# Attention followed by a mixture of experts on one core: tokens as 64 x 9 with 64x64 tiles, engine orders from a list scheduler, experts in three phases

## The chip, the core and the metric

The kernel runs on one core of a Trainium2 chip (trn2). The metric is device time of one execution in microseconds (us), median of the runs. TensorE (PE in the profile, PEld for its weight loads) multiplies matrices, VectorE (DVE), ScalarE (ACT) and GpSimd (POOL) work on tiles, and SyncE (SP) starts transfers. ACT and POOL start transfers too. Inputs lie in DRAM as float32.

## What is computed

```python
def reference(q, k, v, w_gate, w1, w2, capacity):       # q, k, v: [8, 8, 576, 64]
    theta = np.pi / 2 * np.arange(576) / 576
    phi = lambda x: concat(relu(x) * cos(theta), relu(x) * sin(theta))     # 128 features
    kv = einsum('bhsf,bhsd->bhfd', phi(k), v)
    z = phi(k).sum(axis=2)
    num = einsum('bhsf,bhfd->bhsd', phi(q), kv)
    den = einsum('bhsf,bhf->bhs', phi(q), z) + 1e-6
    x = (num / den).transpose(0, 2, 1, 3).reshape(4608, 512)
    logits = x @ w_gate                                  # 8 experts
    e, g = argmax(logits), softmax(logits)[argmax]
    # the first `capacity` (1152) tokens of an expert are kept, in order of the tokens
    out[i] = g[i] * (relu(x[i] @ w1[e[i]]) @ w2[e[i]])   # w1: [8, 512, 1024], w2: [8, 1024, 512]
```

## The kernel before

**Attention and routing.** A pass `it` of the loop at L627 weaves streams of steps that belong to different batches: `stage_a(it)` (L230), `stage_p(it - 1)` (L329) and `stage_r(it - 2)` (L353). `run` (L82) gives every step of a stream a place between two fractions of the pass and issues all steps in the order of these places. This, and nothing measured, sets the order on every engine.

The 576 tokens of a batch are 4 chunks of 128 partitions and a tail of 64. k, v and q are loaded by SP, each as a 128-partition part and a tail (`load`, L187). `stage_a` takes the relu of k on ACT (L242), multiplies v by cos and sin into `vs` (DVE at L257, ACT at L254), transposes the relu of q on TensorE (`q_ps`, L272) and copies the result with ACT to `rq` (L274). `kv_pair` (L291) sums k·v over the 5 chunks, two heads at a time, one in each half of the array's columns:

```python
nc.tensor.matmul(out=kv_v[o * D:(o + 1) * D, w % 2, :, :], lhsT=lhsT, rhs=rhs,          # L301
                 start=(c == 0), stop=(c == NC - 1))
```

k·v is copied to `kvt` and `kva` (L304, L305), turned (L313), multiplied by the gate's weights (`g_ps`, L322) and put beside k·v in `kva`, so that the next product gives attention, denominator and logits at once. `stage_p` does this product in 10 units of a batch, four matmuls each (`p_ps`, L339); ACT takes the cos half times `costab` into `tmp` (L344), DVE adds the sin half times `sintab` into `num` (L346). `p_ps` has two buffers. `stage_r` is a chain of some 20 small DVE operations (denominator, logits, maximum, softmax, one-hot `oh`), with a count of tokens by expert on TensorE (`c_ps`, L434 to L444), and ends in `slot_i`, the row of each token in the DRAM table `xd`, sorted by expert. `emit` (L491) scales `num` into `xg` (3 of 5 chunks on DVE, 2 on POOL) and `scatter` (L500) writes the rows by indirect DMA from POOL.

**Experts.** A table of blocks of 128 rows of one expert is made on DVE: `table_a` after 7 batches for 24 blocks, `table_b` after the last for 19 (L590, L608). `table_b` also makes ACT start 8 small DMAs that write zero rows behind each expert's rows (L614), each after loading a register from `end_i`. `fetch` (L661) reads a block with a transposing DMA (L666) and its token numbers (L668). `up` (L675) multiplies by one half of w1 (`w1a` or `w1b`), ACT takes the relu into `h` (L685), `turn` (L688) transposes `h` on TensorE and DVE copies it to `hT` (L695), `down` (L697) multiplies by w2 (`w_sb`), DVE or ACT copies `y` (two buffers), and POOL scatters its rows to the output (L716).

The halves `w1a` are loaded during attention (`w1_piece`, L517). `w1b` and w2 lie where the attention pools were, and are loaded by POOL after those pools are released (L645) and after the last batch's scatters in POOL's order (L731 to L734). Seven blocks do their first half of `up` while the last batch is routed; the other blocks follow in the loop at L744, which does both `up` halves and both turns of block i and the `down` of block i - 17 in one round. The last 17 `down` stand alone at the end.

## Time and profile before

| what | value |
|---|---|
| median of 3 runs | 463.3 us (461.96 to 466.05) |
| profiled execution | 467.96 us |
| its span in the trace | 466.2 us |
| busy: PE, DVE, ACT, POOL | 344.4, 182.4, 191.6, 130.0 us |
| mean granted clock of TensorE | 0.871 of 2.4 GHz |

The profile is of one execution. Busy time is the union of an engine's instructions; matmuls are pipelined and their ends are modelled, so the distance between starts says more than a duration. In a timeline row the first number is the start, the second the length of the merged stretch, `x8` the number of instructions, and the brackets hold the idle time before it and what ended it. A float32 matmul is two instructions in the trace, so one unit of P is `x8`.

### The profile page before, as it was taken

What the parts mean: (1) busy time and instruction counts of PE and PEld (TensorE: products, weight loads), DVE (VectorE), ACT (ScalarE), POOL (GpSimd) and SP (SyncE); (2) the same over time, 40 slices, a digit from 0 to 9 for tenths busy, and PEclk for the clock granted to TensorE, in tenths of its full rate; (3) what the DMA queues carried; (4) which work ended last, traced back from release to release, by engine and by line L of the source; (5) the groups of instructions that cost most, each with busy time, mean ns of one, the idle gap of its engine ahead of it and who ended that gap; (6) DMA issues with size and microseconds to landing.
All of it is one profiled execution on the core that took longest, in us unless ns stands there. A gap on an engine that the chain in (4) does not pass through costs nothing.

```text
span 466.2 us, 8117 instructions
## 1 busy us (share of the span) xinstructions
PE 344.4 (74%) x2651; PEld 219.6 (47%) x2672; DVE 182.4 (39%) x528; ACT 191.6 (41%) x367; POOL 130.0 (28%) x157
## 2 busy tenths in 40 slices
PE   0079779798988878956560049753999999999984
PEld 0066557576767666754220024431455555555331
DVE  1131356746575757548490002210223232323221
ACT  1064776756757676632110015431343434342110
POOL 3000001615160617256075320000222222223444
PEclk9986997959797989885575559998899999999999
DMA  1975472867877774452249999999455332111220
GB/s 25 337 249 167 140 226 80 252 150 211 192 230 172 221 181 79 73 102 65 64 113 172 213 207 188 186 197 175 93 123 105 103 103 79 69 69 70 99 93 35
DMA packets 91560, 66.55 MB, mean 143 GB/s; under 512 B 46077, under 2 KB 88061, under 8 KB 91520
## 3 DMA queue, kind: packets, MB, share of 16 engines
q0 software_dynamic: 22000, 30.96, 30.7%
q1 hardware_dynamic: 68368, 34.01, 29.5%
q10 hardware_dynamic: 1152, 1.05, 0.8%
q8 instruction: 24, 0.39, 0.4%
q14 instruction: 16, 0.13, 0.1%
HBM read 61.92 MB, written 17.06 MB: 169 GB/s over the span
## 4 chain that ended last, share of the span: by engine, by line
PE 49%; DMA 20%; DVE 8%; issue 7%; ACT 7%; POOL 3%; SPq 3%; another core or an unknown queue 1%; POOLq 0%; DVEq 0%; ACTq 0%
PE h_ps L683 13%; PE kv_ps L301 10%; PE y_ps L704 10%; PE p_ps L339 8%; DMA xT<-xd 7%; DMA w1b<-in_moe_w_dram 5%; DMA out_dram<-y,ix 4%; PE ht_ps L694 3%; DVE num L346 2%; ACT vs L254 2%; PE q_ps L272 2%; ACT tmp L344 2%; DMA qm<-in_q_dram 2%; PE g_ps L322 2%; DMA qt<-in_q_dram 2%
## 5 line engine op out<-in xcount | busy, mean ns | idle before, releaser
L685 ACT ACTIVATE h<-h_ps 128x512 bf16<-128x512 f32 x86 | 51.3, 598 | 120.3 <-PE h_ps L683 103.2
L704 PE MATMUL y_ps<-w_sb,hT 128*128 x333 | 80.5, 385 | 11.4 <-DMA w_sb<-in_moe_w_dram 6.6
L339 PE MATMUL p_ps<-kva,rq 64*128 64x146 f32 (+1 forms) x640 | 75.2, 353 | 8.8 <-DVE num L346 6.8
L695 DVE COPY hT<-ht_ps 128x512 bf16<-128x512 bf16 x86 | 33.0, 420 | 120.6 <-PE ht_ps L694 111.7
L683 PEld LDWEIGHTS <-xT 128*128 128x128 bf16 x344 | 34.4, 101 | 72.3 <-issue 28.2
L346 DVE SCALAR_TENSOR_TENSOR num<-p_ps,sintab,tmp 128x292 f32<-128x292 f32 (+1 forms) x80 | 41.3, 518 | 69.5 <-ACT tmp L344 63.8
L339 PEld LDWEIGHTS p_ps<-kva,rq 64*128 64x128 f32 (+1 forms) x640 | 55.0, 212 | 22.5 <-DVE num L346 12.5
L683 PE MATMUL h_ps<-w1a,xT 128*128 x166 | 47.4, 406 | 15.9 <-DMA xT<-xd 10.6
L495 POOL TENSOR_TENSOR xg<-num,rden 128x512 bf16<-128x512 f32 x16 | 18.0, 1128 | 144.3 <-DVE rden L488 144.1
L716 POOL DMA_INDIRECT out_dram<-y,ids x24 | 23.4, 975 | 122.6 <-DVE y L710 87.6
L683 PE MATMUL h_ps<-w1b,xT 128*128 x168 | 45.1, 391 | 16.8 <-issue 16.6
L344 ACT ACTIVATE tmp<-p_ps,costab 128x292 f32<-128x292 f32 (+1 forms) x80 | 40.1, 501 | 40.4 <-PE p_ps L339 37.3
L704 PEld LDWEIGHTS <-hT 128*128 128x128 bf16 x344 | 32.9, 99 | 47.2 <-issue 14.5
L503 POOL DMA_INDIRECT xd<-xg,slot_i x40 | 44.3, 1108 | 22.7 <-DVE xg L495 13.7
L301 PE MATMUL kv_ps<-vs,km 128*64 128x130 f32 x512 | 43.7, 322 | 1.7 <-ACT vs L254 1.7
L272 PE MATMUL q_ps<-ident,qr 128*128 128x128 f32 x128 | 25.1, 334 | 23.4 <-DVE qr L214 23.4
L694 PE MATMUL ht_ps<-identb,h 128*128 128x128 bf16 x344 | 28.4, 224 | 14.3 <-ACT h L685 14.3
L301 PEld LDWEIGHTS kv_ps<-vs,km 128*64 128x64 f32 x512 | 34.3, 162 | 8.2 <-issue 4.8
L694 PEld LDWEIGHTS <-h 128*128 128x128 bf16 x344 | 24.0, 100 | 27.5 <-ACT h L685 15.4
L710 DVE COPY y<-y_ps 128x512 f32<-128x512 f32 x22 | 15.2, 692 | 49.7 <-PE y_ps L704 28.8
L708 ACT COPY y<-y_ps 128x512 f32<-128x512 f32 x21 | 12.3, 587 | 48.6 <-DMA out_dram<-y,ix 25.1
L272 PEld LDWEIGHTS q_ps<-ident,qr 128*128 128x128 f32 x128 | 17.7, 172 | 25.9 <-issue 23.7
(142 smaller groups left out, 329.9 us busy)
## 6 DMA issues: line engine op xcount, KB each, us to landing
km<-in_k_dram SPq DMA_DIRECT2D x8, 1024.0 KB
vm<-in_v_dram SPq DMA_DIRECT2D x8, 1024.0 KB
qm<-in_q_dram SPq DMA_DIRECT2D x8, 1024.0 KB
w_sb<-in_moe_w_dram POOLq DMA_DIRECT2D x8, 1024.0 KB
w1a<-in_moe_w_dram POOLq DMA_DIRECT2D x8, 512.0 KB
w1b<-in_moe_w_dram POOLq DMA_DIRECT2D x8, 512.0 KB
xd<-zrow ACTq DMA_DIRECT2D x8, 128.5 KB
kt<-in_k_dram SPq DMA_DIRECT2D x8, 128.0 KB
```

The lines of the kernel that those rows point to most:

```text
L272: nc.tensor.transpose(out=q_ps[:, j, :], in_=qr[:, w, j, :, :].rearrange("p o d -> p (o d)"), identity=ident[:])
L301: nc.tensor.matmul(out=kv_v[o * D:(o + 1) * D, w % 2, :, :], lhsT=lhsT, rhs=rhs, start=(c == 0), stop=(c == NC - 1))
L339: nc.tensor.matmul(out=p_ps[0:rows, o, r, 0:2 * KW], lhsT=rq[o * D:(o + 1) * D, 2 * u + r, c * P:c * P + rows], rhs=kva[o * D:(o + 1) * D, ...
L344: nc.scalar.activation(out=tmp[0:rows], in_=p_v[0:rows, :, 0:KW], func=ACT.Copy, scale=costab[0:rows, c:c + 1])
L346: nc.vector.scalar_tensor_tensor(out=num[0:rows, c, u * HB:(u + 1) * HB, :], in0=p_v[0:rows, :, KW:2 * KW], scalar=sintab[0:rows, c:c + 1] ...
L503: si = nc.gpsimd.indirect_dma_start(out=xd[:, :], out_offset=bass.IndirectOffsetOnAxis(ap=slot_i[0:rows, c:c + 1], axis=0), in_=xg[0:rows, ...
L683: nc.tensor.matmul(out=h_ps[:], lhsT=bl["xT"][:, g, :], rhs=w1h[n][:, bass.ds(e1, 1), g, :], start=(g == 0), stop=(g == G - 1))
L685: nc.scalar.activation(out=h[:], in_=h_ps[:], func=ACT.Relu)
L694: nc.tensor.transpose(out=t_ps[:, f, :], in_=bl["h", n][:, f * P:(f + 1) * P], identity=identb[:])
L695: nc.vector.tensor_copy(out=bl["hT"][:, n * (FB // 2):(n + 1) * (FB // 2), :], in_=t_ps[:])
L704: nc.tensor.matmul(out=y_ps[:], lhsT=bl["hT"][:, f, :], rhs=w2_sb[:, bass.ds(e2, 1), f, :], start=(f == 0), stop=(f == FB - 1))
L716: oi = nc.gpsimd.indirect_dma_start(out=out[:, :], out_offset=bass.IndirectOffsetOnAxis(ap=idx, axis=0), in_=y[:], in_offset=None, bounds_ ...
```

## The change

**Layout.** A batch is 64 partitions x 9 consecutive tokens (`J = 9`), and the two halves of the 128 partitions hold two heads. A load row is 9 tokens of one head, 2304 bytes; there is no tail. SP loads v, then k, then q, each in two halves, and `wg_sb` goes to ACT's queue.

**k·v.** The contraction is over 64 partitions and the output has 64 rows, so a matmul uses a quarter of the array; the four heads of a half batch take the four quarters in turn, 9 steps each, 72 matmuls (144 instructions) for a batch in place of 40 (80).

**P.** Still 10 units of four matmuls. The factor cos is divided out: ACT copies the cos half unscaled, DVE adds the sin half times tan, and the 1e-6 is scaled by 1/cos. There are three buffers of two banks for P and k·v, three for `tmp`, two single banks for the rest, two buffers each for `vs`, `rq`, `kva`, `num`, `xg` and the routing tiles, and three for `y`.

**Order.** Every step becomes an `op` of a `Plan` with engine, cost, reads, writes, buffers and a priority. `schedule` simulates the engines with these written costs and takes, on the engine that can start first, the ready op of least priority within a window; table `PHI` shifts the priority by kind of step. The program is emitted in the order found.

**Experts.** The fetch is a plain DMA of 128 rows (`xr`, 4 buffers) which TensorE transposes (`xturn`) and DVE copies (`xT`); POOL copies the token numbers (`ids`). Phase one is `xturn`, `up` with `w1a` and `turn` of all 43 blocks, phase two `up` with `w1b` and `turn`, phase three all 43 `down`. w2 is in two halves: the first is loaded with `w1b` once the last P is through (`swap`), the second into the place of `w1a`, once phase one is done.

```diff
-            m = pl.tile([P, H, NJ, D], FP32, name=name + "m", tag=name + "m")
-            t = pl.tile([D, H, D], FP32, name=name + "t", tag=name + "t")
-            nc.sync.dma_start(out=m[:], in_=src[b, :, 0:NJ * P, :].rearrange("h (p j) d -> p h j d", j=NJ))
-            nc.sync.dma_start(out=t[:], in_=src[b, :, NJ * P:S, :].rearrange("h p d -> p h d"))
+        src = srcs[name][b].rearrange("(u c o) (p j) d -> u (o p) c (j d)", u=2, o=2, j=J)[u]
...
+            nc.sync.dma_start(out=m.rearrange("p c j d -> p c (j d)"), in_=src)
+        op("SP", 0.5, f, w=[(name, b, u)], vers=[vm], prio=b - 1.2, dma=1.55).tag = ("load", name, b, u)
...
+        def kv_half(u):
+            def f():
+                kv_v = kv_tile()
+                for j in range(J):
+                    for c in range(2):
+                        for o in range(2):
+                            nc.tensor.matmul(out=kv_v[c * D:(c + 1) * D, o, u, :, :],
+                                             lhsT=loaded[b, "k", u].tile[o * D:(o + 1) * D, c, j, :],
+                                             rhs=vs_t[vs.slot][o * D:(o + 1) * D, 2 * u + c, j, :, :],
+                                             start=(j == 0), stop=(j == J - 1))
...
+            op("PE", 2.0, kv_half(u), r=[("rk", b, u)] + [("vs", b, j) for j in range(J)], w=[("kvps", b)],
+               vers=[kv, kva, loaded[b, "k", u], vs], prio=pr, mode="quad").tag = ("KV", b, u)
...
+                nc.scalar.copy(out=t[0:rows], in_=p_v[0:rows, :, 0:KW])
...
+                op("PE", 0.51, f, r=[("rq", b, u), ("kva", b)], w=[("pps", b, c, u)], vers=[pv, num, rq[u], kva],
+                   prio=pr - 0.1, mode="row").tag = ("P", b, c, u)
+                op("ACT", 0.32, g, r=[("pps", b, c, u)], w=[("tmp", b, c, u)], vers=[pv, tmp], prio=pr - 1,
+                   ).tag = ("tmp", b, c, u)
+                op("DVE", 0.44, h, r=[("pps", b, c, u), ("tmp", b, c, u)], w=[("num", b)], vers=[pv, tmp, num],
+                   prio=pr - 1).tag = ("num", b, c, u)
...
+            o = op("ACT", 0.95, s_pad(e), r=[("end",)], prio=prio, dma=0.4)
...
-        ti = nc.sync.dma_start(out=xT[:], in_=xd[bass.ds(r0, P), 0:DT], transpose=True)
+            early_read(nc.sync.dma_start(out=xr[:], in_=xd[bass.ds(row(SP), P), :]))
...
+                nc.tensor.transpose(out=x_ps[:, g * P:(g + 1) * P], in_=xrv.tile[:, g * P:(g + 1) * P],
+                                    identity=identb[:])
...
+        for m in range(2):
+            pm = pr + 60 * m
+            op("PE", 0.88, f_up(m), r=[("xT", i), ("w1", m)], w=[("h", i, m)], vers=[xv, pvs[m]], prio=pm, mode="full",
+               ).tag = ("up", i, m)
...
+            pd = pr + 120
...
+    for e in range(E):
+        w1_load(1, e, 50.0 + e, [swapped])
+    for e in range(E):
+        w2_load(0, e, 60.0 + e, [swapped])
+    downs = [block(i) for i in range(NBLK)]
+    for e in range(E):
+        w2_load(1, e, 70.0 + e, [o for o in ops_of("up") if o.tag[2] == 0])
+    for down in downs:
+        down()
+    plan.schedule()
+    plan.emit()
```

On TensorE in the middle of attention a pass of before alternates P of one batch with k·v of the next. Before:

```order
L281 MATMUL qt_ps_941<-ident_66,qrt_552 128x64 x4
L339 MATMUL p_ps_952<-kva_549,rq_548 128x146 x4
L301 MATMUL kv_ps_962<-vs_173,km_536 64x130 x8
L301 MATMUL kv_ps_962<-vs_173,kt_537 64x130 x2
L339 MATMUL p_ps_976<-kva_549,rq_548 128x146 x4
```

Now, at the same place, the count of the batch before (its last row), the turn, the q transposes and gates, then P without a break, then all of k·v of the next batch:

```order
L663 MATMUL a1_891<-oh1_882,onest_160 128x8
L498 MATMUL a0_913<-ident_83,kvt0_886 128x128 x4
L433 MATMUL a1_930<-ident_83,qr0_884 128x128 x4
L512 MATMUL a0_939<-wg_sb_132,tsb0_924 128x32 x4
...
L539 MATMUL p2_999<-kva0_918,rq0_946 128x146 x4
L539 MATMUL p0_1007<-kva0_918,rq0_946 128x146 x4
...
L539 MATMUL p2_1086<-kva0_918,rq1_988 128x146 x4
L469 MATMUL p0_1096<-vs1_80,km2_576 64x130 x36
L469 MATMUL p0_1096<-vs1_80,km3_600 64x130 x36
```

The P units have moved together: ten stand in a row (seven are left out above), and the k·v that stood between them follows them in two groups.

On ACT where attention ends and the experts begin, before did five blocks' relu ahead of the zero rows (`L614`):

```order
L344 ACTIVATE tmp_2362<-p_ps_2357,costab_93 64x292
L407 ACTIVATE ex_2394<-dl_2393 128x40
L685 ACTIVATE h_2437<-h_ps_2438 128x512
...
L685 ACTIVATE h_2574<-h_ps_2575 128x512
L612 TENSOR_LOAD end_i_2581
L614 ISA
L614 DMA xd_63<-zrow_82 128x514
```

Now (`L859` is the zero rows, `L959` the relu of `h`):

```order
L546 COPY tmp1_2645<-p0_2632 128x292
L612 ACTIVATE ex1_2701<-dl1_2687 128x40
L857 TENSOR_LOAD endb_2762
L859 ISA
L859 DMA xd_63<-zrow_163 128x514
...
L959 ACTIVATE h0_2869<-p1_2750 128x512
L959 ACTIVATE h1_2876<-p2_2777 128x512
```

The eight register loads and DMAs (seven are left out) now stand ahead of the first relu of any block.

## Rows read from the trace of the kernel before

**Rows 1.** Busy time by stage, columns as named in the first line.

```profile
core 0: us, PE busy (x) PEld busy (x) DVE busy (x) ACT busy (x) POOL busy (x), PEclk, DMA share, GB/s
...
43.40:223.20 179.80, 148.43 (x1512) 116.56 (x1511) 111.29 (x312) 114.40 (x234) 62.86 (x64) 0.84 0.61 162
223.20:280.00 56.80, 18.77 (x95) 9.40 (x98) 17.75 (x64) 6.61 (x12) 20.95 (x23) 0.58 0.89 155
280.00:424.50 144.50, 128.55 (x786) 66.69 (x800) 37.35 (x89) 52.48 (x88) 24.37 (x25) 0.98 0.63 122
```

**Rows 2.** Chain that ended last, in order of time: start, us, what.

```profile
62.35 1.09 PE g_ps L322 x8
...
179.26 1.09 PE g_ps L322 x8
...
359.65 1.73 PE h_ps L683 x8
...
361.83 1.73 PE y_ps L704 x8
```

**Rows 3.** Timeline of TensorE in one pass of attention.

```profile
117.89 0.25 PE L441 MATMUL c_ps<-oh,onesb 128*128 128x16 bf16 x4
118.08 0.18 PE L443 MATMUL c_ps<-oh,ub 64*128 64x8 bf16 x1
...
125.14 1.11 PE L301 MATMUL kv_ps<-vs,km 128*64 128x130 f32 x16
126.18 0.44 PE L301 MATMUL kv_ps<-vs,kt 64*64 64x130 f32 x4
126.55 0.77 PE L339 MATMUL p_ps<-kva,rq 64*128 64x146 f32 x8
127.25 1.11 PE L301 MATMUL kv_ps<-vs,km 128*64 128x130 f32 x16
```

**Rows 4.** Timeline of TensorE in the experts.

```profile
273.98 3.57 PE L683 MATMUL h_ps<-w1b,xT 128*128 x8 [16.57 <-issue]
...
292.80 0.61 PE L694 MATMUL ht_ps<-identb,h 128*128 128x128 bf16 x8
293.24 1.03 PE L683 MATMUL h_ps<-w1a,xT 128*128 x4
```

**Rows 5.** Groups by line and shape: busy us, mean ns, idle before, releasers.

```profile
L346 DVE SCALAR_TENSOR_TENSOR num<-p_ps,sintab,tmp 128x292 f32<-128x292 f32 x64 | 33.2, 520 | 63.7 <-ACT tmp L344 62.5 <-ACT rq L274 1.2
L344 ACT ACTIVATE tmp<-p_ps,costab 128x292 f32<-128x292 f32 x64 | 32.1, 501 | 34.7 <-PE p_ps L339 32.7 <-DVE qr L214 1.6
L214 DVE TENSOR_SCALAR qr<-qm 128x1024 f32<-128x1024 f32 x16 | 17.4, 1101 | 25.6 <-DMA qm<-in_q_dram 25.6
L495 DVE TENSOR_TENSOR xg<-num,rden 128x512 bf16<-128x512 f32 x16 | 11.4, 744 | 0.1
L222 DVE TENSOR_SCALAR qrt<-qt 64x256 f32<-64x256 f32 x16 | 4.3, 310 | 0.0
```

**Rows 6.** Instructions on the tile kv_ps: ns min/median/max.

```profile
L301 PEld LDWEIGHTS kv_ps<-vs,km x512: 132/137/231, 27.6 to 198.5; 128*64 128x64 f32 x171
```

**Rows 7.** Timeline of ACT behind the last batch.

```profile
240.80 14.76 ACTq L614 DMA_DIRECT2D xd<-zrow  x8
```

**Rows 8.** Timeline of DVE, table of the last blocks, first and last operation of 24.

```profile
239.20 0.15 DVE L584 SCALAR_TENSOR_TENSOR cib<-carry,base 128x8 int32<-128x8 f32 x1
...
244.77 0.28 DVE L574 TENSOR_SCALAR penb<-nvb,prow 128x19 int32<-128x19 f32 x1
```

**Rows 9.** Timeline at the end of the program, last `down` products.

```profile
437.57 3.61 PE L704 MATMUL y_ps<-w_sb,hT 128*128 x16 [0.22 <-DVE y L710]
...
441.41 3.61 PE L704 MATMUL y_ps<-w_sb,hT 128*128 x15 [0.22 <-DVE y L710]
```

**Rows 10.** Timeline of the first load and its first reader.

```profile
8.84 0.60 SPq L195 DMA_DIRECT2D km<-in_k_dram  x1
...
15.11 1.06 ACT L242 ACTIVATE km<-km 128x1024 f32<-128x1024 f32 x1 [11.94 <-DMA km<-in_k_dram]
```

More of the change, by code (lines that the diff above doesn't have):

```diff
@@ new lines @@
+    for t, tab in ((0, cosn), (1, sinn)):
+      for vs in vs_t:
+        nc.gpsimd.tensor_copy(out=vs[:, :, :, t, D], in_=tab[:].unsqueeze(1).to_broadcast([P, HB, J]))
+    for t_ in num_t:
+        nc.gpsimd.memset(t_[D:P, NJ, :, :], 1.0)
+    wg_sb = const.tile([P, 4, 2, 2, E], FP32, name="wg_sb")
+    nc.vector.memset(wg_sb[:], 0.0)
+    wg_v = moe_w_gate.rearrange("(u c o d) e -> o u d c e", u=2, c=2, o=2)
+    for t in range(2):
+        for w in range(4):
+            nc.scalar.dma_start(out=wg_sb[t * D:(t + 1) * D, w, t, :, :], in_=wg_v[w // 2, w % 2])
@@ new lines, in t_out, with g_view, gates @@
+        def t_out():
+            t = tl(tsb, [P, 4, P], FP32, "early")
+            nc.scalar.copy(out=t[:].rearrange("p w x -> p (w x)"), in_=tv.tile[:])
+        def g_view():
+            return tl(gv, [P, 512], FP32, "ps")[:, 0:16 * E].rearrange("p (o u t c e) -> p o u t c e", u=2, o=2, t=2, c=2)
+        def gates():
+            g_v = g_view()
+            for w in range(4):
+                o, u = w // 2, w % 2
+                nc.tensor.matmul(out=g_v[:, o, u, :, :, :], lhsT=tsb.tile[:, w, :], rhs=wg_sb[:, w, :, :, :],
+                                 start=True, stop=True)
@@ L655 @@
[L655 to L670 removed]
+                                in_=moe_w1[e].rearrange("(g p) f -> p g f", p=P)[:, :, n * FH:(n + 1) * FH])
@@ new lines, in f_up, with f, f_relu @@
+        def f_up(m):
+            def f():
+                e1 = expert()
+                hp = tl(pvs[m], [P, 2, 512], FP32, "ps")[:, 0, :]
+                for g in range(G):
+                    nc.tensor.matmul(out=hp, lhsT=xv.tile[:, g, :], rhs=w1h[m][:, bass.ds(e1, 1), g, :],
+                                     start=(g == 0), stop=(g == G - 1))
+            return f
+        def f_relu(m):
+            def f():
+                h = tl(hvs[m], [P, 2, 2, P], BF16, "moe")
+                nc.scalar.activation(out=h[:], in_=pvs[m].tile[:, 0, :].rearrange("p (g q i) -> p g i q", g=2, i=2),
+                                     func=ACT.Relu)
+            return f
@@ new lines, in block, with swap @@
+        return down
+    for b in range(B):
+        for name in "vkq":
+            for u in range(2):
+                load(b, name, u)
+        attention(b)
+    def swap():
+        early.release()
+        pools["mid"] = ctx.enter_context(tc.tile_pool(name="mid", bufs=1))
+    swapped = op("POOL", 0.01, swap, after=[o for o in plan.ops if o.tag[0] in ("num", "tmp", "P") and o.tag[1] == B - 1],
+                 prio=-50)
+    swapped.tag = ("swap",)
+    for b in range(B):
+        routing(b)
+        if b == BA - 1:
+            tab_ops("a", NA, BA, b + 0.3)
@@ new lines, with swap2 @@
+    tab_ops("b", NB, B, B + 0.3)
+    def swap2():
+        late.release()
+        pools["end"] = ctx.enter_context(tc.tile_pool(name="end", bufs=1))
+    swapped2 = op("POOL", 0.01, swap2, prio=-50, after=[swapped] + [
+        o for o in plan.ops if o.tag[0] in ("R", "xg", "scat", "pos", "carry") and o.tag[1] == B - 1] + [
+        o for o in plan.ops if o.tag[0] in ("tab", "end")])
+    swapped2.tag = ("swap2",)
+    for s, gate in [(s, swapped) for s in range(U0, U0 + U1)] + [(s, swapped2) for s in range(U0 + U1, uS.n)]:
+        taken = Ver(uS)
+        taken.uses.append(gate)
+        uS.holder[s] = taken
```

1206 lines of the change are left out of this document (676 added, 530 removed).

## Prediction

> **What bounds the kernel now.** Read the busy times by stage first [rows 1]. There are four stages. Attention, from the first P at 43.4 to the last at 223.2, has TensorE busy 148 of 180 us at a clock of 0.84, with DVE and ACT at about 112 us each: TensorE is nearly the bound, but no engine is full. Then come 56.8 us in which TensorE is busy 18.8 us at a clock of 0.58: a hole. Then 144.5 us of experts at a clock of 0.98, where TensorE is the bound, and at the end some 42 us in which the last `down` products go out. Next, the chain that ended last gives the pace [rows 2]: the same step of two batches, five apart, at 62.35 and 179.26, so 23.4 us for a batch; and in the experts 1.73 us for the eight matmuls of `up` and 1.73 for the eight of `down`. The timelines then say what fills the hole and the end: 14.76 us in which ACT does nothing but start eight small DMAs [rows 7], TensorE waiting 16.57 us before the first product with `w1b` and then running at half pace [rows 4], and two `down` in 3.84 us at the end, where 3.46 would do, because two `y` buffers wait for their stores [rows 9].
>
> **The change part by part.**
>
> *Start.* SP no longer sends eight `wg_sb` DMAs first; its first load goes out near 1 us and not at 8.84. That load was read 6.3 us after its issue [rows 10], so v is there near 8, k near 12. ACT then has eight products of v and two relus of k, about 6 us, and TensorE works at the low clock: k·v, turns and gates to about 32, ten units of P to 39. I take 39 for the last P of the first batch; 34 to 44 are its bounds.
>
> *A batch in steady state.* The chain is read off the new orders. After the last P, TensorE does k·v of the next batch and the count; DVE, which was waiting for the count, finishes the routing, takes a relu of q, scales v for the batch after, makes `xg`, and only then adds up the next P units, of which three can be waiting.
> - k·v, 144 instructions. Two tiles at a time now start an instruction each 65 ns: 16 in 1.04 us [rows 3]. No row shows four at a time. If four overlap as two do, the pace is half, 33 ns (4.7 us); if only two overlap, 65 ns (9.4 us); if nothing overlaps and each waits for its own weight load of 135 ns [rows 6], 19.4 us. The shortest pace of a weight load and matmul in the trace is that of the small count matmuls, four in 0.19 us, 47 ns [rows 3]. I take that: 6.8 us.
> - the count with its handover: 0.75 us.
> - DVE: eight small operations at 0.24 us (24 of the table take 5.85 us [rows 8]), 1.95; a relu of q at 1.10 x 1152/1024, 1.24; ten products of v with 256 columns at 0.31, 3.1; three `xg` at about 0.72, 2.16 [rows 5]. Together 8.45 us.
> - ten P units. The loop through three buffers is P 0.5, ACT about 0.5, DVE 0.52 and some 0.35 of handover [rows 3, 5], 1.9 us for three, so 0.63 a unit; from DVE's start to the last P on TensorE, 5.0 us.
>
> The sum is 21.0 us, where 23.4 are taken now. P is shorter on TensorE (0.70 us a unit between k·v groups [rows 3], and at least 0.5 when units follow each other), but this lies under DVE and I count nothing for it. ACT, with 114 us of work in these 180 now [rows 1], is covered. Loads, weights and scatter are the same bytes in fewer and longer rows; transfers used 0.61 of the engines at 23.4 us a batch [rows 1], so about 0.68 at 21, and I count nothing. If that cover fails, TensorE waits for k or v at the start of its group.
>
> The Trainium skill speaks against this part: TensorEngine Tiling (Array Packing), section PSUM Bottleneck, says that tiles speed up the products and not the copying of their results. By that rule no pace of the tiles brings a batch under what DVE needs. Here that is 17.9 us, from [rows 5, 8]: P 5.2, v 3.1, two relus 2.5, some 20 routing operations, 4.9, and `xg` 2.2. The sum above stays over it.
>
> *The last pass* has the first table, 18 operations, 4.3 us, and no products of v, minus 3.1: 22.2 us. So the last P ends at 39 + 6 x 21.0 + 22.2 = 187, where it is 223 now.
>
> *The hole.* The first blocks need the table and the scatters of batch 7 and come 3.5 us after the last P. TensorE can then turn four blocks and do two `up` (2.6 us) until it needs a relu. On ACT the eight zero-row DMAs stand ahead of the first relu, and wait for the last count, at about 5.5. Eight took 14.76 us beside heavy weight loads [rows 7]; with fewer loads beside them they can be quicker, which no row shows. Half of it is the lower bound; I take 11, the middle. So the first relu comes at 16.5. On DVE, queued behind the same count, are the rest of the routing (1.5), `xg` (2.2) and the whole second table (5.85), so the third block's copy comes at 15. TensorE works without a break from 18 us after the last P. The bounds are 10 and 25.
>
> *The experts.* Each block costs 1.73 + 1.73, eight turns in 0.44 [rows 2, 4], and now four more turns, 0.22, for the transposing DMA that goes: 4.12 us, 177.2 for 43 blocks, less the 2.6 done. That it is TensorE work again is the price of 9.5 us for fetches that don't stall. The first eight matmuls after the hole cost 1.7 us more, as the row after the 16.57 us wait shows, and I add 2.5 for fetches that come late beside the weight loads: 4.2. `w1b` and half of w2 have the 56 us of phase one to arrive in, and the rest of w2 the 47 us of phase two, so no wait is counted for weights. In phase three, three `y` buffers at a cycle of 3.84 us each allow a store every 1.28 us, less than 1.73: the stores are hidden. The end behind the last `down` is as now, 5.1 us.
>
> *Sum.* 187.2 + 18 + 174.6 + 4.2 + 5.1 = 389 us of span. The profiled execution has 1.8 us outside its span and is 467.96 against a median of 463.3. So 391 in the same measure, and 387 for the median.
>
> **The rivals.**
> - *Smoother* (365). Four tiles at 33 ns and quick zero rows. For it: half the pace of two tiles is just 33. Against it: no row shows instructions that close together. k·v is 2.1 us shorter but routing then comes later than the count; 1.9 a batch, 15 in eight, and 7 in the hole.
> - *Two at a time* (408). 65 ns: 2.6 us more a batch, 21 in all. For it: this is the only pace that k·v shows now, also in its 64*64 rows. Against it: nothing in the trace says what limits that pace.
> - *The hole stays* (417). Fetches and zero rows compete with 8.4 MB of weights. For it: in the hole now, where this happens, transfers use 0.89 of the engines [rows 1]. Against it: the weights are now spread over phase one. A block in phase one then takes 1.9 us and not 1.3, 26 us, and the `w1b` wait some more: 30.
> - *Low clock* (457). In every batch TensorE would wait some 4 us behind the DVE chain, the 8.45 us less the turns and gates that fit in it; granted 1.2 GHz throughout, k·v takes 13.6 us, P in the burst 1.5 more, the count 0.5: 8.8 a batch, 70 in all. Against it: in attention now, with waits as well, the granted clock is 0.84 [rows 1]. The Trainium skill, TensorE: Matmul & The Clock Gate, section "HAM oscillation — how this bites in real kernels", says that a kernel whose bursts are parted by waits falls back in each of them; by that rule this would be the outcome, and the 0.84 speaks for a part of it only.
> - *Slower than before* (488). The 64x64 tiles don't overlap: each instruction waits for a weight load of 135 ns [rows 6], k·v takes 19.4 us, 12.6 more a batch, 101 in all. It becomes slower than now when an instruction takes more than about 114 ns (the 77 us of span between 389 and 466, over eight batches of 144). Against it: tiles of half the array overlap now, at 65 ns with weight loads of 135.
>
> **How the numbers follow.** Forecast 387: 0.51, with 372 to 402 as its own range. Smoother 0.25, two at a time 0.10, the hole stays 0.08, low clock 0.03, slower 0.03. The range from 350 to 422 leaves out the last two and the edges of the others. Faster by more than 1% (about what a measurement of this kernel can tell from no change) are all but the last: 0.96. Within 1%: 0.01, for a place between the last two. Slower: 0.03.
>
> **What would show it.** In the changed profile: the gates' product of two batches 21 us apart; 72 k·v matmuls in 6.8 us; the last P at 187; ACT's eight zero-row DMAs ahead of the first relu, and TensorE idle behind them for some 12 us; then TensorE full at a clock near 1, a `down` each 1.73 us with no wait for a store. The prediction is wrong if a batch takes over 23 us, if DVE has idle time in attention while TensorE is full, if phase one takes over 65 us, or if phase two or three waits for weights.

## The result and the profile after

The changed kernel takes 417.1 us (median of four runs, 414.4 to 420.0), the kernel before 463.3 beside it: a ratio of 0.900 with a 95% interval of 0.892 to 0.907. The profiled execution took 414.44 us with a span of 412.6. A second set of four runs gave 420.6 us and 0.904 [0.897, 0.912]. The forecast was 387, its range 350 to 422; the result lies in the range, at the place that the rival "the hole stays" named, 417.

The stages of the kernel after (columns as named in the first line): up to the end of the last P of the first batch; up to the end of the last P of all; the hand-over and phase one up to where TensorE runs without a break; the rest of phase one, whose last product with `w1a` ends at 284.1, together with phase two; and phase three:

```profile
core 0: us, PE busy (x) PEld busy (x) DVE busy (x) ACT busy (x) POOL busy (x), PEclk, DMA share, GB/s
0.00:44.20 44.20, 17.54 (x259) 14.98 (x260) 18.70 (x73) 21.11 (x46) 4.51 (x20) 1.00 0.82 266
44.20:186.40 142.20, 116.48 (x1879) 102.53 (x1879) 124.77 (x322) 94.28 (x215) 61.68 (x62) 0.88 0.63 179
186.40:262.50 76.10, 49.52 (x370) 27.03 (x369) 37.78 (x114) 17.85 (x31) 25.02 (x55) 0.91 0.95 187
262.50:330.40 67.90, 67.59 (x504) 38.76 (x504) 28.98 (x84) 33.62 (x57) 7.70 (x19) 1.00 0.42 83
330.40:405.20 74.80, 74.65 (x348) 33.74 (x347) 15.30 (x24) 12.74 (x22) 41.34 (x42) 1.00 0.34 127
```

Against [rows 1]: the last P ends at 186.4 and not at 223, and from there to the end it takes 226 us where it took 243. In attention DVE is busy 125 of 142 us and has become the bound; TensorE is down from 148 to 116. From 262.5 on TensorE is full, at a granted clock of 1.00. What is left is one bad stage: in the 76 us from 186.4 to 262.5 TensorE is busy 49.5, with transfers at 0.95.

Timeline of TensorE in one batch (start, length, merged instructions, idle time before and what ended it); the first row answers to the k·v rows of [rows 3]:

```profile
102.97 4.24 PE L469 MATMUL p<-vs,km 64*64 64x130 f32 x144
107.26 0.25 PE L656 MATMUL a<-oh,mlt 128*128 128x40 bf16 x4
...
113.21 1.76 PE L539 MATMUL p<-kva,rq 64*128 64x146 f32 x24
117.87 4.42 PE L539 MATMUL p<-kva,rq 64*128 64x146 f32 x56 [2.90 <-DVE num L551]
122.22 4.24 PE L469 MATMUL p<-vs,km 64*64 64x130 f32 x144
```

and of DVE beside it:

```profile
108.49 0.15 DVE L674 TENSOR_TENSOR carry<-a,carry 128x8 f32<-128x8 f32 x1
...
110.16 1.34 DVE L423 TENSOR_SCALAR qr<-qm 128x1152 f32<-128x1152 f32 x1
111.43 0.34 DVE L407 TENSOR_SCALAR vs<-vm,cosn 128x256 f32<-128x256 f32 x1
111.69 3.90 DVE L407 TENSOR_SCALAR vs<-vm,sinn 128x256 f32<-128x256 f32 x9
115.51 1.88 DVE L724 TENSOR_TENSOR xg<-num,rden 128x512 bf16<-128x512 f32 x3
117.31 1.36 DVE L551 SCALAR_TENSOR_TENSOR num<-p,tant,tmp 64x292 f32<-64x292 f32 x3
...
126.25 0.20 DVE L623 TENSOR_TENSOR oh<-key,kmx 128x40 bf16<-128x40 f32 x1
```

Of the nine products in the row of 3.90 us, eight take about 0.34 us each and one takes 1.80; beside that one POOL works on its part of `xg`:

```profile
112.21 1.80 DVE L407 TENSOR_SCALAR vs<-vm,sinn 128x256 f32<-128x256 f32 x1
112.79 1.06 POOL L724 TENSOR_TENSOR xg<-num,rden 128x512 bf16<-128x512 f32 x1
```

This batch, from k·v to k·v, is 19.25 us, and its chain can be read from the starts: k·v 4.24, the count and its way to DVE (107.21 to 108.49) 1.28, DVE from the count to its first sum 8.82, from there to the last P 4.91. Four tiles take an instruction each 4.24/144 = 29 ns.

The hand-over to the experts, first on TensorE:

```profile
187.57 0.77 PE L932 MATMUL a<-identb,xr 128*128 128x128 bf16 x8 [1.17 <-DMA xr<-xd]
...
204.01 1.01 PE L967 MATMUL a<-identb,h 128*128 128x128 bf16 x8 [8.25 <-DVE un L936]
```

on ACT, where the zero rows answer to [rows 7]:

```profile
193.16 6.89 ACTq L859 DMA_DIRECT2D xd<-zrow  x8
200.10 1.08 ACT L959 ACTIVATE h<-p 128x512 bf16<-128x512 f32 x2 [9.97 <-DMA xd<-zrow]
```

and on DVE, where `xg` and the table answer to [rows 5, 8]:

```profile
193.71 2.75 DVE L724 TENSOR_TENSOR xg<-num,rden 128x512 bf16<-128x512 f32 x3
196.38 0.15 DVE L782 SCALAR_TENSOR_TENSOR cib<-carry,base 128x8 int32<-128x8 f32 x1
...
203.40 0.24 DVE L847 TENSOR_SCALAR penb<-nvb,prow 128x19 int32<-128x19 f32 x1
203.55 0.75 DVE L936 COPY un<-a 128x512 bf16<-128x512 bf16 x2
```

The relus are out by 201.2, but TensorE goes on only at 204.0, when DVE has been through `xg` and the whole second table (196.38 to 203.55). Two of DVE's operations there are long, and POOL works on `xg` beside both: the second `xg` takes 1.54 us where the others take about 0.7, and one operation of the table 1.75 where its neighbours take about 0.2.

Phase one, TensorE, two blocks of a group of four that repeats (L952 is `up`, L967 the turn of `h`, L932 the turn of the fetched rows):

```profile
237.76 0.39 PE L967 MATMUL a<-identb,h 128*128 128x128 bf16 x4
238.25 1.02 PE L952 MATMUL p<-w1a,un 128*128 x4
239.11 0.39 PE L967 MATMUL a<-identb,h 128*128 128x128 bf16 x4
239.33 0.39 PE L932 MATMUL a<-identb,xr 128*128 128x128 bf16 x4
240.02 0.40 PE L967 MATMUL a<-identb,h 128*128 128x128 bf16 x4 [0.30 <-ACT h L959]
240.84 1.02 PE L952 MATMUL p<-w1a,un 128*128 x4 [0.43 <-issue]
242.62 0.40 PE L967 MATMUL a<-identb,h 128*128 128x128 bf16 x4 [0.75 <-ACT h L959]
```

At 241.9 an `up` ends, and the next thing in TensorE's written order is the turn of that same `up`'s result, so TensorE stands for ACT's relu, 0.75 us. A group of four blocks takes 8.4 us (237.76 to 246.17, where the pattern begins again), 2.1 us a block.

### The profile page after: what moved, and what is told of

The parts are those of the page before. It is cut to its first block, busy times and chain, and to the rows that moved or that the text cites. A ratio compares the mean times of both kernels' runs of the same rounds, so it can differ in the third digit from the quotient of the medians.

```text
span 412.6 us, 9632 instructions
## 1 busy us (share of the span) xinstructions
PE 325.8 (79%) x3356; PEld 217.0 (53%) x3356; DVE 226.2 (55%) x613; ACT 179.6 (44%) x369; POOL 141.2 (34%) x199
## 3 DMA queue, kind: packets, MB, share of 16 engines
q0 software_dynamic: 18032, 30.96, 33.8%
q10 hardware_dynamic: 2304, 1.09, 1.1%
## 4 chain that ended last, share of the span: by engine, by line
PE 41%; DVE 27%; DMA 12%; issue 7%; ACT 6%; POOL 4%; SPq 1%; POOLq 1%; ACTq 0%; DVEq 0%
PE p L952 16%; PE p L993 10%; DMA xr<-xd 7%; PE p L539 6%; DVE vs L407 6%; DVE qr L423 4%; POOL out_dram L1010 4%; PE a L967 4%; DVE num L551 3%; DMA vm<-in_v_dram 3%; DVE xg L724 3%; ACT vs L405 2%; PE p L469 2%; PE a L932 2%; ACT tmp L546 1%
## 5 line engine op out<-in xcount | busy, mean ns | idle before, releaser
L959 ACT ACTIVATE h<-p 128x512 bf16<-128x512 f32 x86 | 51.2, 597 | 89.4 <-PE p L952 79.5
L993 PE MATMUL p<-w,un 128*128 x344 | 74.6, 379 | 0.1
L973 DVE COPY un<-a 128x512 bf16<-128x512 bf16 x86 | 36.3, 424 | 69.5 <-PE a L967 69.5
L539 PE MATMUL p<-kva,rq 64*128 64x146 f32 x640 | 56.7, 329 | 15.4 <-DVE num L551 14.0
L539 PEld LDWEIGHTS p<-kva,rq 64*128 64x128 f32 x640 | 50.1, 218 | 21.7 <-DVE num L551 19.1
L993 PEld LDWEIGHTS <-un 128*128 128x128 bf16 x344 | 33.6, 98 | 40.4 <-issue 0.4
L551 DVE SCALAR_TENSOR_TENSOR num<-p,tant,tmp 128x292 f32<-128x292 f32 (+1 forms) x80 | 39.2, 514 | 28.3 <-ACT tmp L546 28.0
L733 POOL DMA_INDIRECT xd<-xg,si x40 | 44.6, 1115 | 26.6 <-DVE xg L724 16.8
L952 PEld LDWEIGHTS <-un 128*128 128x128 bf16 x344 | 32.7, 98 | 31.5 <-issue 9.2
L952 PE MATMUL p<-w1a,un 128*128 x172 | 45.5, 392 | 3.4 <-issue 1.5
L469 PEld LDWEIGHTS p<-vs,km 64*64 64x64 f32 x1152 | 33.7, 139 | 24.6 <-issue 23.6
L724 POOL TENSOR_TENSOR xg<-num,rden 128x512 bf16<-128x512 f32 x16 | 17.5, 1093 | 79.8 <-DVE rden L700 74.6
L952 PE MATMUL p<-w1b,un 128*128 x172 | 44.0, 378 | 0.0
L967 PE MATMUL a<-identb,h 128*128 128x128 bf16 x344 | 33.3, 221 | 13.6 <-DVE un L936 8.3
L967 PEld LDWEIGHTS <-h 128*128 128x128 bf16 x344 | 25.1, 98 | 33.8 <-ACT h L959 17.6
L433 PE MATMUL a<-ident,qr 128*128 128x128 f32 x144 | 27.9, 326 | 12.2 <-DVE qr L423 5.5
```

The source lines that it names most:

```text
L469: nc.tensor.matmul(out=kv_v[c * D:(c + 1) * D, o, u, :, :], lhsT=loaded[b, "k", u].tile[o * D:(o + 1) * D, c, j, :], rhs=vs_t[vs.slot][o * ...
L539: nc.tensor.matmul(out=p_ps[:, a, o, 0:2 * KW], lhsT=rq[u].tile[a * D:(a + 1) * D, o, col:col + P], rhs=kva.tile[a * D:(a + 1) * D, o, u, ...
L551: nc.vector.scalar_tensor_tensor(out=num.tile[0:rows, c, u * HB:(u + 1) * HB, :], in0=p_v[0:rows, :, KW:2 * KW], scalar=tant[0:rows, c:c + ...
L733: si = nc.gpsimd.indirect_dma_start(out=xd[:, :], out_offset=bass.IndirectOffsetOnAxis(ap=xg.si[0:rows, c:c + 1], axis=0), in_=xg.tile[0:r ...
L952: nc.tensor.matmul(out=hp, lhsT=xv.tile[:, g, :], rhs=w1h[m][:, bass.ds(e1, 1), g, :], start=(g == 0), stop=(g == G - 1))
L959: nc.scalar.activation(out=h[:], in_=pvs[m].tile[:, 0, :].rearrange("p (g q i) -> p g i q", g=2, i=2), func=ACT.Relu)
```

## Experiments

The last three columns are read from the profiled execution of each run. "P to end" is from the end of the last P to the end of the span, which takes attention out; "experts" is from where TensorE goes on behind the hand-over's wait for DVE's first copies (204.01 above) to the last `down`, which ends where the copy of its `y` begins. Each ratio is to the kernel before, run beside on the same chip; h1_both ran on another chip than the other experiments. The stages of g1_tab are left out. Where the text says control, it means f0_after.

| run | what | median us | ratio and 95% interval | last P ends | P to end | experts |
|---|---|---|---|---|---|---|
| after, first | the change | 417.1 | 0.900 [0.892, 0.907] | 186.4 | 226.2 | 201.1 |
| f0_after | the change again | 420.6 | 0.904 [0.897, 0.912] | 193.4 | 224.0 | 198.9 |
| e1_thin | 14 weight loads less | 414.3 | 0.885 [0.882, 0.889] | 191.2 | 221.6 | 199.1 |
| e2_plan | plain repetition in phase one | 412.8 | 0.883 [0.881, 0.885] | 192.1 | 218.8 | 193.6 |
| h1_both | both | 396.2 | 0.851 [0.845, 0.856] | 192.2 | 203.8 | 181.3 |
| e6_w2late | half of w2 later | 406.6 | 0.870 [0.866, 0.873] | 192.7 | 211.8 | 186.7 |
| e3_wg | `wg_sb` on POOL | 407.9 | 0.872 [0.869, 0.875] | 181.7 | 225.4 | |
| f1_two_tiles | two tiles at a time | 436.8 | 0.936 [0.928, 0.944] | 211.6 | 226.7 | |
| f2_reluq | a relu of q on ACT | 413.8 | 0.889 [0.882, 0.896] | 184.8 | 226.5 | |
| f3_all | three edits | 388.3 | 0.832 [0.825, 0.839] | 175.7 | 213.9 | |
| g1_tab | f3, table later | 392.8 | 0.840 [0.833, 0.846] | | | |
| g3_tabdense | g1, plain repetition | 396.4 | 0.847 [0.841, 0.853] | 183.4 | 214.1 | |
| g2_meas | f3, measured costs | 397.2 | 0.849 [0.843, 0.856] | 186.3 | 212.6 | |

### Phase one: transfers, the written order, or both

Theory A: fetches come late beside the weights. Theory B: TensorE's order, written with the planner's costs, holds the stalls itself.

**e1_thin**: the same order, without 14 of 16 weight loads.

```diff
     def w1_load(n, e, prio, after):
         def f():
+            if n == 1 and e > 0:
+                return
...
-                    nc.tensor.matmul(out=hp, lhsT=xv.tile[:, g, :], rhs=w1h[m][:, bass.ds(e1, 1), g, :],
+                    nc.tensor.matmul(out=hp, lhsT=xv.tile[:, g, :], rhs=w1h[m][:, 0:1, g, :] if m else w1h[m][:, bass.ds(e1, 1), g, :],
```

The same is done for the first half of w2 (left out above).

> Left out: seven of the eight loads of w1b and of the first half of w2 (each product of those halves reads expert 0's weights), so 14 loads of 512 KB are gone from phase one; the order of every engine in phase one is word for word that of the changed kernel. After it now, 27 blocks of phase one take 57 us from 205 to 262, 2.1 us each, where TensorE needs 1.3. Theory A (transfers: fetches come late beside the weights): the pace falls to about 1.4, the 27 blocks end some 19 us earlier, 398 us in all. Theory B (the written order itself holds the stalls: a turn stands right behind the product whose relu it needs, up(i), then turn(i), with nothing between): only the waits for fetched rows go, 9 us by the waits (PE L932 behind xr: 5.1 + 4.1), and 408 us are left. Both: between.

**e2_plan**: the same loads, another order in phase one (in attention TensorE, DVE and ACT keep theirs).

```diff
+    DMA_W = 1.4
...
-        op("POOL", 0.85, f, w=[("w1", n)], prio=prio, dma=2.95, after=after).tag = ("w1", n, e)
+        op("POOL", 0.85, f, w=[("w1", n)], prio=prio, dma=DMA_W, after=after).tag = ("w1", n, e)
...
-        op("POOL", 0.95, f, w=[("w2", n)], prio=prio, dma=2.8, after=after).tag = ("w2", n, e)
+        op("POOL", 0.95, f, w=[("w2", n)], prio=prio, dma=DMA_W, after=after).tag = ("w2", n, e)
```

> The same loads and bytes; only the planner is told that a weight load takes 1.4 us of the transfers and not 2.95 or 2.8, and so it writes phase one as a plain repetition: turn of the next rows, up, turn back, block by block, where it wrote groups of four blocks with waits in them. Theory A (transfers hold phase one): the same pace, 415 to 419 us. Theory B (the written order holds it): the waits for h and un within the groups go, 15.7 us by the waits (PE and PEld L967 behind ACT h: 5.3 + 10.4) and phase one falls from 2.1 to about 1.5 us a block: 400 us.

Neither came near what its theory alone would give: e1_thin is 16 us above theory A's 398, e2_plan 13 above theory B's 400. First e1_thin, TensorE's waits for relus in the stretch from 210 to 262 (group, what it waited for: us, times, longest), and the busy times of that stretch:

```profile
PE a L971 <- ACT h L963: 4.9, 11, 0.8
...
PEld L971 <- ACT h L963: 9.6, 18, 1.2
```

```profile
210.00:262.00 52.00, 41.97 (x303) 23.00 (x308) 20.55 (x57) 15.52 (x26) 4.61 (x25) 0.96 0.24 63
```

The same two views of e2_plan, where the waits are for fetched rows:

```profile
PE a L933 <- DMA xr<-xd: 4.4, 4, 2.1
...
PEld L933 <- DMA xr<-xd: 5.9, 6, 2.3
```

```profile
210.00:262.00 52.00, 43.67 (x335) 25.89 (x340) 22.95 (x67) 16.16 (x28) 13.76 (x40) 0.93 1.04 204
```

Without the weights there is no wait for a fetched row, and transfers (the last column but one) fall to 0.24 of the engines from 1.01 in the control; but the waits for relus stay where the order put them, 4.9 us before products (4.3 in the control, 5.3 in the first profile of the changed kernel). With the plain order no wait for a relu is left, but there are 4.4 us of waits for fetched rows (1.6 in the control, 4.1 in the first profile), with transfers at 1.04. The row of PE and the row of PEld show the same idle time twice, once before the product and once before its weight load, so they do not add: in e1_thin TensorE is idle for 10.0 of the 52 us in all. Both expectations added them; the 15.7 us that theory B hoped for were 5.3 us before products.

**h1_both** puts the two edits together.

> Both halves of the first two experiments at once: the order with the plain repetition (1.4 us for a weight load in the plan), and 14 of the 16 loads of w1b and of the first half of w2 left out (every product of those halves reads expert 0's weights). From the last P to the end the changed kernel takes 224.0 us (193.4 to 417.4 in its second run), 221.1 without the loads, 218.4 with the plain repetition. If the two causes are separate stalls that add, 224.0 - 2.9 - 5.6 = 215.5. If each hides behind the other (where one stall goes, the other is already waiting), the pace comes to the 1.3 to 1.4 us a block that TensorE needs: 27 blocks at 0.7 us less, 19 us, 205.

Its timeline of TensorE in phase one (L937 turns the fetched rows, L957 is `up`, L972 turns `h`):

```profile
217.25 0.39 PE L937 MATMUL a<-identb,xr 128*128 128x128 bf16 x4
217.47 1.03 PE L957 MATMUL p<-w1a,un 128*128 x4
218.34 0.39 PE L972 MATMUL a<-identb,h 128*128 128x128 bf16 x4
218.56 0.39 PE L937 MATMUL a<-identb,xr 128*128 128x128 bf16 x4
218.78 1.03 PE L957 MATMUL p<-w1a,un 128*128 x4
```

A block each 1.31 us, no wait; 203.8 us from the last P, where the second reading said 205. On the experts alone the edits give -0.2, 5.3 and together 17.6 us. So phase one has two limits at nearly the same height, and each hides behind the other.

**e6_w2late**: eight loads move from phase one to its last blocks and phase two, and the planner then also writes phase one in the plain order.

```diff
+    for o in ops_of("w2", 0):
+        d = ops_of("up", 34 + o.tag[2], 0)[0]
+        o.deps.append(d)
```

> The first half of w2, which only phase three reads, is loaded behind phase one and not in it (eight loads of 512 KB move to phase two, where transfers are busy 0.42). The planner sees this and writes phase one as turn, up, turn back, block by block. Theory A: half the weights' 8.4 MB leave phase one, fetches come on time, pace 1.4 to 1.5, 397 us. Theory B: the order is as dense as in the run with the cheaper weight loads in the plan, so the same time as that run, within 3 us.

Theory A's side of it holds, 6.2 us better than e2_plan where B allowed 3, though 10 us short of A's 397. The experts take 12.2 us less than in the control, with every weight still loaded: half of these loads in phase one and the plain order.

### The start

**e3_wg**

```diff
-            nc.scalar.dma_start(out=wg_sb[t * D:(t + 1) * D, w, t, :, :], in_=wg_v[w // 2, w % 2])
+            nc.gpsimd.dma_start(out=wg_sb[t * D:(t + 1) * D, w, t, :, :], in_=wg_v[w // 2, w % 2])
```

> The eight small loads of wg_sb are issued on POOL's queue and not on ACT's. In the changed kernel ACT's queue holds them from 4.4 to 18.9 us, so ACT's first product of v starts at 18.98, 11.5 us after DVE's. Theory C (those eight loads hold back ACT and with it the first batch): ACT starts at about 8, the first k.v at 15 to 18 and not at 23.4, the last P of the first batch at 36 to 38 and not 44, and 409 us in all. Rival (k and q come no earlier anyway, because SP's own issues wait): 415 to 417.

ACT's timeline in the changed kernel, with the eight DMAs and what stood behind them:

```profile
4.39 14.54 ACTq L312 DMA_DIRECT2D wg_sb<-in_moe_w_gate_dram  x8
18.98 3.31 ACT L405 ACTIVATE vs<-vm,cosn 128x256 f32<-128x256 f32 x8 [15.26 <-DMA wg_sb<-in_moe_w_gate_dram]
```

In the experiment, POOL's timeline:

```profile
4.71 5.00 POOL L312 DMA_DIRECT2D wg_sb<-in_moe_w_gate_dram  x8
```

and ACT's:

```profile
5.90 3.30 ACT L405 ACTIVATE vs<-vm,cosn 128x256 f32<-128x256 f32 x8 [2.18 <-DMA vm<-in_v_dram]
```

The last P of the first batch ends at 33.8 and not at 44.2, the last P of all 9.5 to 11 us earlier than in e1_thin, e2_plan and e6_w2late, whose orders of TensorE, DVE and ACT in attention are the same (191.2 to 192.7), and from there on little changes (225.4, 224.0 in the control). The gain was larger than the 8 us expected: v was there at 5.9 us, and the relus of k behind ACT's products of v had nothing to wait for.

### Attention: the tiles and DVE

**f0_after** is the changed kernel again, the control.

> The changed kernel as it is, again, so that the experiments of this call stand beside it on the same chip. The ratio to the kernel before was 0.8997 [0.892, 0.907]; the same within that interval is expected of every theory.

**f1_two_tiles**

```diff
-                for j in range(J):
-                    for c in range(2):
+                for c in range(2):
+                    for j in range(J):
                         for o in range(2):
                             nc.tensor.matmul(out=kv_v[c * D:(c + 1) * D, o, u, :, :], ...
```

> The same 144 k.v matmuls a batch, with the loops exchanged, so that only two 64x64 tiles alternate at a time (the two row halves of one column half) and not four. Every other instruction stands where it stood. In the changed kernel four tiles go at 29 ns an instruction, 4.24 us a batch, between 122.2 and 126.5, and the count stands behind them; DVE's eight routing steps from the last sum (123.3) to the one-hot (126.45) go on beside them, so the 4.24 us are just hidden, with one relu of q (1.3 us) as slack. Theory D (the pace of the tiles counts, because DVE waits for the count behind k.v): 65 ns, 9.4 us, of which 5.1 - 1.3 = 3.8 us a batch are not hidden, 7 to 8 times: 27 to 31 us slower, ratio 0.96. Rival (DVE is the bound whatever the tiles do, as it is busy 17.6 of 19.2 us): under 5 us slower, ratio 0.91.

k·v in its timeline of TensorE:

```profile
115.99 7.08 PE L469 MATMUL p<-vs,km 64*64 64x130 f32 x144
...
138.99 7.08 PE L469 MATMUL p<-vs,km 64*64 64x130 f32 x144 [0.57 <-DVE num L551]
```

16 us slower, between the two expectations. Two tiles go at 7.08/144 = 49 ns and not at the 65 that [rows 3] show for before; a batch takes 23.0 us and not 20.7 as in the control. So 2.3 of the 2.84 us are felt: theory D has the mechanism right, with too high a price and too much slack.

**f2_reluq**

```diff
-                nc.vector.tensor_scalar(out=t[:], in0=loaded[b, "q", u].tile[:].rearrange("p c j d -> p j c d"),
-                                        scalar1=0.0, scalar2=None, op0=ALU.max)
+                src = loaded[b, "q", u].tile[:].rearrange("p c j d -> p j c d")
+                if u in Q_ACT:
+                    nc.scalar.activation(out=t[:], in_=src, func=ACT.Relu)
+                else:
+                    nc.vector.tensor_scalar(out=t[:], in0=src, scalar1=0.0, scalar2=None, op0=ALU.max)
```

`Q_ACT` is `(1,)`, and the planner is told of the change (1.1 us on ACT for 0.68 on DVE; left out above).

> One of the two relus of q of each batch is made by ACT and not by DVE (1.34 us a batch off DVE, which is busy 17.6 of 19.2 us; ACT goes from 13.9 to about 15.2). Theory E (DVE sets the batch): a batch takes 1.0 to 1.3 us less, 8 to 10 us in all, ratio 0.88. Rival (the loop from the last sum by the count, routing and gates back to the first product sets it, and ACT's relu now stands in that loop, ahead of the gates' copies): 0 to -3 us, ratio 0.895 to 0.90.

6.8 us less than the control, nearer to theory E. DVE's way from the count to its first sum shrinks from 8.8 to 7.2 us (131.51 to 138.70 in one batch), but the sums behind it then wait more: five times 0.31 to 0.72 us in that burst (three times 0.24 to 0.45 in the changed kernel's from 117.31), three of the five for ACT's copies.

**f3_all** is e6_w2late, e3_wg and f2_reluq together.

> Three edits together: wg_sb on POOL's queue, the first half of w2 loaded behind phase one, one relu of q on ACT. Alone the first measured 0.8721 and the second 0.8695, against 0.8997 of the changed kernel: 0.0276 and 0.0302. If each acts in its own stage (start, phase one, attention) the savings add: 0.842 without the relu, 0.82 to 0.825 if DVE sets the batch. Rival (a gain in one stage is given back in the next, since transfers of the weights wait for the same engines): above 0.855.

388.3 us, 32.3 less than the control; the three alone gave 12.7 and 14.0 (medians against 420.6; the ratios give 15.0 and 16.3) and 6.8. Each gain lies in its own stage, and they nearly add. This version beats both kernels: it is 79 us faster than the kernel before, run beside it.

### The hand-over, and costs in the planner: three misses

**g1_tab** and **g3_tabdense**

```diff
-    tab_ops("b", NB, B, B + 0.3)
+    tab_ops("b", NB, B, 30.0)
-            o = op("ACT", 0.95, s_pad(e), r=[("end",)], prio=prio, dma=0.4)
+            o = op("ACT", 0.95, s_pad(e), r=[("end",)], prio=26.0, dma=0.4)
```

g3_tabdense has the `DMA_W = 1.4` of e2_plan besides; that the priority of `s_end` moves with the zero rows is left out above.

> On top of the three edits together (388.3 us, ratio 0.832): the second block table, which only the last 19 blocks need, and the eight zero-row DMAs get a later priority (30 and 26 in the place of 8.3), so that DVE and ACT do the first blocks' copies and relus ahead of them. In the run of the three edits DVE's first copy for the experts stands at 192.1, 16.4 us after the last P, behind xg (2.75) and the table (7.1). Theory F (DVE's table is what holds TensorE at the hand-over, not the zero rows): TensorE goes on at about 9.5 us after the last P and not at 16.8; 7 us less, ratio 0.817. Rival 1 (the zero rows or the fetches hold it as well): 0 to 3 us less. Rival 2 (the planner, which now has the zero rows among the fetches, writes phase one in groups again, and gives it back as the stalls of theory B): the hand-over is 7 us shorter and phase one as much longer, 0.83.

> The same, and the planner is told 1.4 us for each weight load and not 2.95 or 2.8, which gives phase one the plain repetition again behind the first dozen blocks. Theory F with theory B: the 7 us of the hand-over and no groups, ratio 0.812 to 0.817. If the groups cost nothing, the same as the run without this cost.

The hand-over itself did what theory F says. In g3_tabdense the first five `up` are through 19.6 us after the last P, in f3_all 26.0, and TensorE waits 4.16 us for DVE where it waited 11.08. Yet neither run is faster, and g3_tabdense is slower. In g1_tab the planner wrote phase one in groups again, as the second rival said. In g3_tabdense ACT's zero rows now stand among the relus and hold them up, as its timeline of ACT shows:

```profile
204.20 0.60 ACT L964 ACTIVATE h<-p 128x512 bf16<-128x512 f32 x1 [0.51 <-PE p L957]
204.71 4.56 ACTq L864 DMA_DIRECT2D xd<-zrow  x3
209.36 0.60 ACT L964 ACTIVATE h<-p 128x512 bf16<-128x512 f32 x1 [4.57 <-PE a L937]
```

They are not the largest loss. Between 203 and 245 TensorE's products wait for fetched rows most of all,

```profile
PE a L937 <- DMA xr<-xd: 3.6, 5, 0.9
```

then 1.2 us for relus and 1.1 for the table, while in f3_all, over the same blocks, they wait for no fetched row. At the 29th `up` 0.2 us of the 6.4 are left (its relu starts 61.4 us behind the last P against 61.6), and from the last P to the end nothing: 214.1 against 213.9. The lower cost of a weight load applies to `w1a` too, and with it attention was written worse: the last P came 7.7 us later, with one wait of 9.06 us for a sum that DVE's first table held up. So the table is what holds TensorE at the hand-over, and moving it together with the zero rows was worth nothing in these orders.

**g2_meas** sets 16 costs of the planner to what the profile shows.

> On top of the three edits together: the planner's costs of 16 operations are set to what the profile shows (an ACT copy of a P unit 0.40 for 0.32, a DVE sum 0.52 for 0.44, a product of v on DVE 0.41 for 0.21, a relu of q on DVE 1.34 for 0.68, the routing's steps 0.22 for 0.11, the experts' copies 0.42 for 0.34, the relus 0.62 for 0.5). Theory G (an order written with true costs waits less): a batch 0.5 to 1 us shorter, 4 to 8 us in all, ratio 0.815 to 0.824. Rival (attention is bound by DVE's work, which the order does not change): within 2 us, 0.828 to 0.836.

Wrong, and on the other side: the last P comes 10.6 us later than in f3_all and the rest is nearly the same (212.6). With the true costs the planner splits k·v into two groups with the turns of q between them, so that the count comes later, and DVE waits for it: 4.4 us in four batches between 80 and 160, where f3_all has 0.2. The granted clock of TensorE over attention is lower as well, 0.84 against 0.93, and no run parts the two. Truer costs did not give a better order; a greedy choice under a table of priorities that was made for the other costs gave another one. Whether a table made for the true costs would gain, no run shows.

## Why the prediction was right, and where it was off

It said faster, and the time is in its range, but outside the 372 to 402 that the forecast had as its own, and at the number of a rival that was given 0.08. The last P stands where it was put, 186.4 against 187.2, by luck: two errors cancel. The hand-over came out in time, if not in its way; the experts did not:

| term | predicted | measured |
|---|---|---|
| last P of the first batch | 39 | 44.2 |
| from there to the last P | 148.2 | 142.2 |
| hand-over until TensorE goes on | 18 | 17.6 |
| experts to the last `down` | 178.8 | 201.1 |
| end | 5.1 | 7.4 |
| span | 389 | 412.6 |
| from the profiled run's span to the median | -2 | +4.5 |

*Start*: 39 was too early by 5, just outside its bounds. The step that failed is "ACT then has eight products of v and two relus of k, about 6 us": ACT does take 5.5, but from 18.98 on, because the eight `wg_sb` DMAs that were taken off SP's queue are on ACT's and hold it 14.5 us. The description of the change said so, and only SP's gain was counted. e3_wg shows the price: 10 us. The low clock that was assumed there did not come (1.00 up to 44.2).

*A batch*: 21.0 predicted; from last P to last P the six batches behind the first take 18.6 to 20.4 us, 19.8 on average, and the one shown above 19.25. In that one three of the four terms hold to about half a microsecond: DVE's stretch 8.45 against 8.82, P 5.0 against 4.91, the count 0.75 against 1.28. In DVE's stretch small operations and `xg` were cheaper (1.67 for 1.95 and 1.80 for 2.16), and the ten products of v dearer, 4.08 for 3.1, by the one long product of 1.80 us; the other nine start 0.26 apart. k·v was 6.8 and is 4.24: four tiles overlap as the rival "smoother" had it (33 ns; 29 measured), and the pace of 47 ns, taken from the count matmuls of before, was the term that was mis-sized. The rival "two at a time" read 65 ns off the 64*64 rows as well, but four of those take 0.37 us in [rows 3], 92 ns each. "Smoother" counted its k·v in 365 together with a quicker hole, which did not come. The second set's profile has 20.7 us in its last three batches, with the same 17.5 us of DVE work and more idle time of DVE before its sums (2.6 us for 1.0); why, no run here says.

That DVE sets this stage the prediction had weighed by the Trainium skill, TensorEngine Tiling (Array Packing), section PSUM Bottleneck. The trace agrees: 17.6 busy us of 19.25 in a batch, 17.9 worked out, and with faster products TensorE waits for DVE's sums (2.90 us in the row above). f1_two_tiles adds what the rule leaves open: the products still count as long as DVE waits for something that stands behind them.

*Low clock* did not come as that rival had it, 1.2 GHz throughout: the granted clock over attention is 0.88, where it was 0.84. It came in parts. TensorE waits 2.9 us for DVE's sums in each of three batches in a row. Behind the wait that ends at 117.87 the clock stays at 1.00, and the burst of 56 takes 4.42 us; around the waits that end at 137.10 and 157.42 it is 0.5, which is 1.2 GHz, and the burst of 56 behind the first of them takes 5.50 (rows of the burst, and of two stretches with the columns of the stages above):

```profile
137.10 5.50 PE L539 MATMUL p<-kva,rq 64*128 64x146 f32 x56 [2.88 <-DVE num L551]
136.60:140.00 3.40, 2.90 (x24) 2.90 (x26) 1.86 (x6) 0.81 (x2) 2.79 (x3) 0.50 0.22 77
170.70:184.30 13.60, 10.43 (x70) 9.23 (x71) 11.14 (x27) 4.92 (x13) 7.90 (x8) 0.50 0.40 82
```

In the last pass it is 0.5 for 13.6 us (the last row). The Trainium skill, TensorE: Matmul & The Clock Gate, section "HAM oscillation — how this bites in real kernels", tells of a kernel whose clock falls back in the wait before every burst; the trace agrees in two of these three waits.

*Hand-over*: 18 against 17.6, but by another way. The prediction had ACT's first relu at 16.5 behind 11 us of zero rows and DVE's copy at 15; the zero rows took 6.9, the relu was out by 14.3, and DVE came at 17.1. The mechanism was named; the engine that ended last was the other one, by its two long operations among others.

*Experts*: this is the step that failed, 22 of the 23.6 us of span. The prediction put it as "I add 2.5 for fetches that come late beside the weight loads", on the ground that the weights are spread over phase one. The rival "the hole stays" had the size (a block at 1.9 us, 26 us; measured 2.1) and half of the cause. The other half was in none: the order of TensorE was taken as a list of work, while it is a record of where the planner, with its 2.95 us for each weight load, expected TensorE to wait anyway. h1_both, with both causes gone, takes 181.3 us for the experts (2.0 of them two waits behind "issue" in phase two and three that only the runs with fewer loads have); 178.8 was the sum. The prediction's own sign of being wrong, a phase one of over 65 us, came: from 204.0, where TensorE goes on, to the last product with `w1a` at 284.1 it is 80 us, three blocks of phase two among them. The wait for `w1b` that the rival also named did not come: TensorE is busy 67.6 of 67.9 us from 262.5.

*The rest*: the first eight matmuls behind the hole cost 1.84 us more in [rows 4] (3.57 for 1.73), not 1.7. Stores are hidden in phase three, 74.65 of 74.80 us busy, as predicted. The end is 2.3 us longer: it is 4.8 us from the last `down` in e1_thin and h1_both, the two runs without the 14 loads, and 7.4 to 7.8 in all others; the cause was not looked for. And 6.5 us of the 30 between 387 and 417 are the choice to subtract the 4 us by which the profiled run of before lay above its median, when the one after lay 2.7 below.

## What to carry to other kernels

An order that a planner wrote is data about the planner's costs: a wait that it expected is frozen into the order and stays when the real wait goes, so read the new order for an instruction that stands right behind the one whose result it needs. Where two limits lie at the same height, take both away in one run before calling either harmless: alone they gave 0 and 5 us, together 18. And a step moved off one engine's queue is a step moved onto another's: count what stands behind it there.
